# Putting the raw products of two units side by side in a fast-multiplication GeGLU kernel

## The chip, the cores and the metric

The kernel runs on one core of a Trainium2 chip. The time is microseconds of device time of one execution; the number quoted is the median of several executions. Before the change that was 541.36 us (three runs, 541.24 to 541.87).

## The reference

A gated feed-forward layer on 2048 tokens, all in bf16, with a model width of 1024 and an inner width of 3584:

```python
B, S, Dm, Df = 1, 2048, 1024, 3584
def reference(x, w_gate, w_up, w_down):
    g = jnp.einsum("bsd,df->bsf", x, w_gate)
    u = jnp.einsum("bsd,df->bsf", x, w_up)
    h = _gelu(g) * u                      # gelu with the tanh approximation
    return jnp.einsum("bsf,fd->bsd", h, w_down)
```

## The kernel before

The kernel does each matrix product as a 2x2 block product with seven block products in place of eight (Winograd's form). Two of the seven take the inputs as they are ("raw", bf16 operands). The other five take sums and differences of input blocks, kept in a 32-bit type (`f32r`): `s1`..`s4` and the cast `sa` of the weights, `t1`..`t4` and the cast `tb` of the tokens. The tokens go in two passes of 1024.

In the gate/up stage a "unit" makes 256 inner features of gate and of up. One block product is 2 x 4 matmuls (gate and up, four blocks of the contraction), so a unit is 16 raw and 40 32-bit matmuls, each 128x128 by 512 columns. A unit uses three pairs of PSUM banks (PSUM is the memory that matmuls write). Only unit 0 of the first pass is made plainly, with eight bf16 products. The raw products of the next unit are issued ahead, between this unit's `s4` product and its `sa` product:

```python
def raw_products(e, c, xT, w):
    for i in range(2):
        product(e[i], w[:, i, :KH, :P], [xT[0][:, k, :] for k in range(KH)], True)
    p1 = [snap(e[i], "p1") for i in range(2)]          # ScalarE copies
    for i in range(2):
        b21 = [xT[0][:, KH + k, :] for k in range(KH)]
        product(c[i], w[:, i, KH:, :P], b21, True)
    return p1

def unit(...):                                         # cut to TensorE's order
    product(e[i], s["s2"][i], t["t2"], False)          # each line for i in (0, 1)
    u2 = [snap(e[i], "u2") for i in GU]
    product(c[i], s["s1"][i], t["t1"], True)
    p5 = [snap(c[i], "p5") for i in GU]
    after_p5()                # GpSimd: s1..s4 of the next unit; weight load two ahead
    product(e[i], s["s3"][i], t["t3"], False)
    product(c[i], s["s4"][i], t["tb"], False)
    ahead_of_p4()             # raw products of the next unit
    product(e[i], s["sa"][i], t["t4"], False)
```

In both passes the down stage follows, with 392 matmuls of the same kind (112 bf16, 280 32-bit). One of its helpers fetches raw weights late in the stage:

```python
def fetch73(j):
    raw[3, j] = slot([P, 2, N], bf16, "raw")
    nc.sync.dma_start(out=raw[3, j], in_=wdn[:, :, j, N:])
```

All small tiles share one pool of 52 buffers (`slot`). DMAs are issued by SyncE. TensorE, VectorE, GpSimd and SyncE run in program order; ScalarE's order is chosen by the scheduler, except in the first unit.

Of the kernel before, what the change touches and what calls it, by code (L numbers as in the profile page):

```python
# [1 line left out]

# [8 lines left out]
def kernel(  # L11
# [23 lines left out]
    nc = tc.nc  # L35
    ENG = mybir.EngineType
# [3 lines left out]
    f32 = mybir.dt.float32  # L40
# [3 lines left out]
    ADD, SUB, MUL = ALU.add, ALU.subtract, ALU.mult  # L44
# [9 lines left out]
    NJ = NFB // 2  # L54
    N = 512
    NS = N // P
    NPASS = S // (2 * N)
    NU = NFB // 2
# [21 lines left out]
    wdn = w_down.rearrange("(kh j p) d -> p kh j d", kh=2, p=P)  # L80
# [14 lines left out]
    def new(eng, a, b, op, name, shape=None, dtype=None):  # L95
        t = slot(shape or [P, N], dtype or f32r, name)
        eng(t, a, b, op)
        return t
# [6 lines left out]
    def snap(ps, name):  # L105
        t = slot([P, N], f32, name)
        nc.scalar.copy(out=t, in_=ps)  # L107
        return t
# [8 lines left out]
    def load_w(u, queue=nc.sync):  # L117
        f0 = u * 2 * P
        w = wpool.tile([P, 2, NKB, 2 * P], bf16, name="w")
        for i, src in enumerate((w_gate, w_up)):  # L120
            queue.dma_start(
                out=w[:, i],
                in_=src[:, f0 : f0 + 2 * P].rearrange("(ko ki) f -> ki ko f", ki=P),
            )
        return w
# [38 lines left out]
    def pool_behind(tile):  # L164
        nc.gpsimd.tensor_copy(out=seen, in_=tile[:, :1].bitcast(f32))
# [6 lines left out]
    def make_s(w, eng):  # L172
        s = sums_s(w, eng)
        s.make("s1", "s2", "s3", "sa", "s4")
        return s

    def gelu(src):
        g = slot([P, N], f32, "g")
        nc.scalar.activation(g, src, ACT.Gelu_apprx_tanh)  # L179
        return g  # L180

    def times(fb, c, g, u):
        dve(hT[:, fb // NJ, fb % NJ, c, :], g, u, MUL)
# [14 lines left out]
    def add(ps, other):  # L198
        g = new(dve, ps[0], other[0], ADD, "sum", dtype=f32)
        dve(ps[1], ps[1], other[1], ADD)  # L200
        return g, ps[1]

    def unit(u, banks, xT, w, s, t, c11, after_p5, aside, keep, ahead_of_p4, behind_p4, snap_first):
        GU = range(2)
        e, c, d = banks
        aside(-2)
        g, up = c11()
        aside(-1)
        for i in GU:
            product(e[i], s["s2"][i], t["t2"], False)  # L210
        aside(0)
        keep(0, c[0])
        if snap_first:
            u2 = [snap(e[i], "u2") for i in GU]
            g = gelu(g)
        else:
            g = gelu(g)
        c11 = g, up
        if not snap_first:
            times(2 * u, 0, *c11)  # L220
            u2 = [snap(e[i], "u2") for i in GU]
        keep(1, c[0])
        keep(2, c[1])
        c = d
        for i in GU:
            product(c[i], s["s1"][i], t["t1"], True)
        p5 = [snap(c[i], "p5") for i in GU]
        after_p5()
        for i in GU:
            product(e[i], s["s3"][i], t["t3"], False)  # L230
        g, up = new(dve, e[0], p5[0], ADD, "sum", dtype=f32), banks[1][not snap_first]
        dve(up, e[1], p5[1], ADD)
        if snap_first:
            times(2 * u, 0, *c11)
        for i in GU:
            product(c[i], s["s4"][i], t["tb"], False)
        times(2 * u + 1, 1, gelu(g), up)
        aside(1)
        g, up = add(c, u2)
        ahead_of_p4()  # L240
        for i in GU:
            product(e[i], s["sa"][i], t["t4"], False)
        times(2 * u, 1, gelu(g), up)
        behind_p4()
        times(2 * u + 1, 0, gelu(e[0]), e[1])

# [6 lines left out]
    def fetch_wd(js):  # L253
        big = None
        for j in js:
            if j < NJ - 2:
                wraw[j] = [slot([P, Dm], bf16, "raw") for _ in range(2)]
            else:
                if big is None:
                    big = wpool.tile([P, 4, Dm], bf16, name="w")  # L260
                n = 2 * (j - NJ + 2)
                wraw[j] = [big[:, n + kh] for kh in range(2)]
            for kh in range(2):
                nc.sync.dma_start(out=wraw[j][kh], in_=wdn[:, kh, j, :])

    def keep_part(j, part, ps):
        ra, rb = wraw[j]
        if part == 0:
            made[j] = mpool.tile([P, 3, N], f32r, name="m")
        a = (ra[:, N:], rb[:, N:], rb[:, :N])[part]  # L270
        b = (ra[:, :N], made[j][:, 0], made[j][:, 1])[part]
        nc.scalar.copy(out=ps, in_=a)
        dve(made[j][:, part], ps, b, SUB)

    def keep_whole(j):
        ra, rb = wraw[j]
        m = made[j] = wpool.tile([P, 4, N], f32r, name="w")
        pool(m[:, 0], ra[:, N:], ra[:, :N], SUB)
        pool(m[:, 1], rb[:, N:], m[:, 0], SUB)
        pool(m[:, 2], rb[:, :N], m[:, 1], SUB)  # L280

    def store_made(j):
        nc.sync.dma_start(out=td[:, j], in_=made[j][:, :3].bitcast(f32))
# [28 lines left out]

    def fetch73(j):
        raw[3, j] = slot([P, 2, N], bf16, "raw")
        nc.sync.dma_start(out=raw[3, j], in_=wdn[:, :, j, N:])

    def make73(j):
        rr = raw[3, j]
# [147 lines left out]
    xT = new_x()  # L466
# [4 lines left out]
    w = load_w(1)  # L471
# [58 lines left out]
    def making(u):  # L530
        if u < 2 or u >= NU:
            return []
        return list(range(u - 2, NJ if u == NU - 1 else u - 1))

    for ip in range(NPASS):
        for u in range(1 if ip == 0 else 0, NU):
            js = making(u) if ip == 0 else []

            def prepare():
                nonlocal ahead  # L540
                if first:
                    pool_behind(t["t4"][-1])
                nxt["w"], nxt["s"] = ahead, None
                if u + 1 < NU:
                    nxt["s"] = make_s(ahead, pool)
                if u + 2 < NU:
                    ahead = load_w(u + 2)
                if len(js) == 1:
                    store_made(js[0])
                for j in js[1:]:  # L550
                    keep_whole(j)
                if ip == 0:
                    fetch_wd(making(u + 1))

            def keep(part, ps):
                if js:
                    keep_part(js[0], part, ps)

            def aside(part):
                if (ip, u) == (0, 1) and part < 0:  # L560
                    rest_of_0(part + 2)
                if part == 0 and "t4" not in t:
                    t.make("t4")

            def ahead_of_p4():
                if u + 1 < NU:
                    nxt["p1"] = raw_products(
                        even if u % 2 else odd, cc, xT, nxt["w"]
                    )

            def behind_p4():
                if "p1" in nxt:
                    nxt["c11"] = add(cc, nxt["p1"])

            def c11():
                return nxt.pop("c11", None) or add(cc, p1)

            e = odd if u % 2 else even
            p1 = nxt.pop("p1", None) or raw_products(e, cc, xT, w)
            first = (ip, u) == (0, 1)  # L580
            with tc.manual_schedule(engines={ENG.Activation}) if first else nullcontext():
                unit(
                    u, (e, cc, dd), xT, w, s, t, c11, prepare, aside, keep,
                    ahead_of_p4, behind_p4, first,
                )
            if u + 1 < NU:
                w, s = nxt["w"], nxt["s"]

        last = ip == NPASS - 1
        got, nxt = {}, {}  # L590

        def more(step):

            nonlocal ahead
            if last:
                return
            if step in (-1, 0, 2):
                store_made({-1: NJ - 3, 0: NJ - 2, 2: NJ - 1}[step])
            if step == 0:
                xT[:] = new_x()  # L600
            if step >= 24 and step % 2 == 0 and step // 2 - 12 < len(moves):
                c, ko = moves[step // 2 - 12]
                transposing(xT, c, ko, (2 * (ip + 1) + c) * N)
            if step == 50:
                got["w"], ahead = load_w(0), load_w(1)
            if step == 58:
                got["s"] = make_s(got["w"], dve)
            if step == 62:
                got["t"] = make_t(xT)

        down(ip, even + cc, dd + odd, last, more)
        even, odd, cc, dd = odd, even, dd, cc
        if not last:
            w, t, s = got["w"], got["t"], got["s"]

# [1 line left out]
_INS = ['x', 'w_gate', 'w_up', 'w_down']  # L617
# [26 lines left out]
```

## Time and profile before

| | before |
|---|---|
| time, median | 541.36 us |
| span of the profiled run | 539.9 us |
| PE (matmul) busy | 533.1 us, 99% |
| PEld (weight load) busy | 381.4 us, 71% |
| VectorE, ScalarE, GpSimd busy | 62%, 48%, 44% |
| waits of TensorE | one, 1.2 us at the start |

The first lines are from the page of the kernel before: part 1 (busy time, share, instructions) and part 4 (the chain that ended last).

```profile
PE 533.1 (99%) x2380; PEld 381.4 (71%) x2414; DVE 334.6 (62%) x524; ACT 260.0 (48%) x463; POOL 239.2 (44%) x215
...
PE 99%; issue 0%; ACT 0%; DVE 0%
```

TensorE is the bound. But a busy PE is not a PE at its peak, as matmuls overlap; the Trainium skill ("Perfetto Trace Analysis", section "Identifying the Most-Contended Engine") says the same and sends the reader to the share of peak FLOPs and that of weight loads (71% here). So look at the period. This is the chain of the kernel before in order of time (start us, length us, what):

```profile
82.92 0.07 issue
82.99 12.49 PE bank L111 x55
95.48 0.07 issue
95.55 12.49 PE bank L111 x55
108.04 0.07 issue
```

A unit takes 12.56 us. (x55 is not 56: this trace lacks 34 of 2414 matmul records, most of them the first bf16 matmul behind 32-bit ones. The 2414 weight loads are complete.) The timeline of PE shows the order within two units: start us, length us, operands, count.

```profile
145.79 3.40 PE L111 MATMUL bank<-xT,w 128*128 128x512 bf16 x15
148.84 2.19 PE L111 MATMUL bank<-t,sa 128*128 128x512 f32 x8
150.86 5.60 PE L111 MATMUL bank<-t,s 128*128 128x512 f32 x24
156.30 1.98 PE L111 MATMUL bank<-tb,s 128*128 128x512 f32 x8
158.35 3.40 PE L111 MATMUL bank<-xT,w 128*128 128x512 bf16 x15
161.40 2.19 PE L111 MATMUL bank<-t,sa 128*128 128x512 f32 x8
```

Each unit changes type twice: to bf16 ahead of `xT,w`, and back to 32-bit ahead of `t,sa`. Look at the two groups of eight: `tb,s` takes 1.98 us and `t,sa`, behind the change of type, 2.19 us. The start of the first record after a change is early, so the true cost is smaller than this difference; it comes from the spacing of starts in the single records, in the prediction below.

The weight loads by shape (count, busy us, mean ns, idle us) show where the two types part:

```profile
L111 PEld LDWEIGHTS bank<-t,s 128*128 128x128 f32 x648 | 121.6, 188 | 25.6
L111 PEld LDWEIGHTS <-w 128*128 128x128 bf16 x504 | 47.2, 98 | 58.2 <-issue 6.8
```

A 32-bit weight load takes 188 ns, a bf16 one 98 ns. The Trainium skill ("TensorE: Matmul & The Clock Gate", section "Weight-path perf modes — Fast Weight Load (FWL) and DoubleRow") states that the fast weight load is on for 128 weights of a type that is not FP32, measured at about 2x; this trace, which calls the 32-bit type f32, agrees with 1.9x.

### The profile page before, as it was taken

Reading aid. Unit: us, or ns where it says so; the run is one execution under the profiler, and the core shown is the slowest. Engines: PE = TensorE matmul, PEld = TensorE weight load, DVE = VectorE, ACT = ScalarE, POOL = GpSimd, SP = SyncE. Lnnn points to the kernel's source line nnn. Section 1 sums busy time; section 2 is a strip of 40 time slices with the busy share of each in tenths; the row PEclk is TensorE's granted clock in tenths of the full one; section 3 lists DMA queues with packets and bytes.
Section 4 is the critical chain, followed back from the end, with each engine's and each line's share of the span. In section 5 each row is a group of like instructions: output and inputs, shape, how many; then the busy total and the mean of one; then the engine's idle time right before and its main releaser. Section 6 shows DMA issues by size and latency. Waiting matters only on the chain.

```text
span 539.9 us, 7400 instructions
## 1 busy us (share of the span) xinstructions
PE 533.1 (99%) x2380; PEld 381.4 (71%) x2414; DVE 334.6 (62%) x524; ACT 260.0 (48%) x463; POOL 239.2 (44%) x215
## 2 busy tenths in 40 slices
PE   9999999999999999999999999999999999999997
PEld 5577777766777746888876767777777775488885
DVE  2986666666666895594945445555544459676730
ACT  2566666666666410255355555555555541114431
POOL 1169966677774400000097777777766600000000
PEclk9999999999999999999999999999999999999999
DMA  9776666766654899979673232233330079373751
GB/s 242 159 183 177 175 176 204 197 185 199 200 168 170 294 352 303 302 193 305 225 195 79 78 80 78 79 87 101 100 90 15 1 209 385 126 239 93 232 188 49
DMA packets 108134, 93.28 MB, mean 173 GB/s; under 512 B 17217, under 2 KB 92993, under 8 KB 108097
## 3 DMA queue, kind: packets, MB, share of 16 engines
q1 hardware_dynamic: 108096, 92.82, 59.4%
q8 instruction: 19, 0.31, 0.3%
q14 instruction: 19, 0.15, 0.1%
HBM read 74.45 MB, written 15.20 MB: 166 GB/s over the span
## 4 chain that ended last, share of the span: by engine, by line
PE 99%; issue 0%; ACT 0%; DVE 0%
PE bank L111 97%; PE bank L500 1%; PE bank L447 1%; ACT st L411 0%; DVE warm L431 0%
## 5 line engine op out<-in xcount | busy, mean ns | idle before, releaser
L93 POOL TENSOR_TENSOR s<-w 128x512 fp32r<-128x512 bf16 x102 | 119.9, 1196 | 166.2 <-DVE t L90 87.7
L111 PE MATMUL bank<-t,s 128*128 128x512 f32 x648 | 151.7, 390 | 0.0
L111 PEld LDWEIGHTS bank<-t,s 128*128 128x128 f32 x648 | 121.6, 188 | 25.6
L90 DVE TENSOR_TENSOR hT<-g,bank 128x512 bf16<-128x512 f32 x112 | 75.5, 685 | 67.7 <-ACT g L179 51.1
L107 ACT COPY p<-bank 128x512 f32<-128x512 f32 x124 | 70.5, 591 | 94.9 <-PE bank L111 94.8
L111 PE MATMUL bank<-xT,w 128*128 128x512 bf16 (+1 forms) x476 | 106.2, 375 | 1.9
L111 PEld LDWEIGHTS <-w 128*128 128x128 bf16 x504 | 47.2, 98 | 58.2 <-issue 6.8
L90 DVE TENSOR_TENSOR sum<-bank,p 128x512 f32<-128x512 f32 x54 | 37.1, 687 | 51.4 <-PE bank L111 51.4
L111 PE MATMUL bank<-q 128*128 128x512 f32 x240 | 58.9, 389 | 0.0
L111 PE MATMUL bank<-t,sa 128*128 128x512 f32 x216 | 58.7, 413 | 0.0
L93 POOL TENSOR_TENSOR s<-w,s 128x512 fp32r<-128x512 bf16 x50 | 57.8, 1181 | 0.0
L93 POOL TENSOR_TENSOR s<-s,w 128x512 fp32r<-128x512 f32 x50 | 57.0, 1160 | 0.0
L179 ACT ACTIVATE g<-sum 128x512 f32<-128x512 f32 x81 | 51.1, 630 | 8.5 <-DVE sum L90 7.4
L111 PE MATMUL bank<-tb,s 128*128 128x512 f32 x216 | 53.3, 389 | 0.0
L111 PEld LDWEIGHTS bank<-q 128*128 128x128 f32 x240 | 45.0, 188 | 9.4
L111 PE MATMUL bank<-raw,hT 128*128 128x512 bf16 x218 | 48.4, 379 | 0.3
L111 PEld LDWEIGHTS bank<-t,sa 128*128 128x128 f32 x216 | 40.7, 188 | 10.6
L107 ACT COPY u<-bank 128x512 f32<-128x512 f32 x62 | 35.9, 590 | 24.2 <-PE bank L111 21.8
L111 PEld LDWEIGHTS bank<-tb,s 128*128 128x128 f32 x216 | 40.5, 188 | 8.4
L102 ACT CAST tb<-raw 128x512 fp32r<-128x512 bf16 x28 | 17.2, 626 | 60.2 <-DMA raw<-in_w_down_dram 26.7
L90 DVE TENSOR_TENSOR q<-hT 128x512 fp32r<-128x512 bf16 x56 | 38.3, 685 | 4.1 <-PE bank L111 4.1
L179 ACT ACTIVATE g<-bank 128x512 f32<-128x512 f32 x31 | 18.6, 601 | 46.0 <-PE bank L111 45.7
(45 smaller groups left out, 464.0 us busy)
## 6 DMA issues: line engine op xcount, KB each, us to landing
raw<-in_w_down_dram SPq DMA_DIRECT2D x80, 256.0 KB, 4.8
q<-td SPq DMA_DIRECT2D x60, 256.0 KB, 4.9
w<-in_w_gate_dram SPq DMA_DIRECT2D x27, 512.0 KB, 5.9
w<-in_w_up_dram SPq DMA_DIRECT2D x27, 512.0 KB, 7.0
td<-m SPq DMA_DIRECT2D x12, 768.0 KB, 4.5
w<-td SPq DMA_DIRECT2D x6, 1024.0 KB, 9.8
out_dram<-st SPq DMA_DIRECT2D x32, 128.0 KB, 1.7
td<-w SPq DMA_DIRECT2D x2, 768.0 KB, 6.8
```

The source lines that it names most:

```text
L90: nc.vector.tensor_tensor(out=out, in0=a, in1=b, op=op)
L93: nc.gpsimd.tensor_tensor(out=out, in0=a, in1=b, op=op)
L102: nc.scalar.copy(out=t, in_=src)
L107: nc.scalar.copy(out=t, in_=ps)
L111: nc.tensor.matmul(ps, lhsT=lhs, rhs=rhs, start=start, stop=stop, skip_group_check=True)
L179: nc.scalar.activation(g, src, ACT.Gelu_apprx_tanh)
L447: nc.tensor.transpose(tp[:, ko, :], xn[i][:, ko * P : (ko + 1) * P], ident)
L500: nc.tensor.matmul(bank[3][:, :cols], lhsT=warm[:, :P], rhs=warm[:, :cols], start=True, stop=True)
```

## The change

The intent: issue the raw products of two units side by side, every other unit, so that TensorE changes type half as often. That needs a fourth pair of banks, so the pairs rotate (`E, K, C, F`). The raw weights must be there earlier, so their load moves ahead in the unit. ScalarE takes the program's order in the whole of gate/up. And two late fetches of each pass are split into two DMAs each. The core of the diff, with cuts marked:

```diff
@@ unit
-        if not snap_first:
-            times(2 * u, 0, *c11)
 ...
         g, up = add(c, u2)
+        times(2 * u, 1, gelu(g), up)
         ahead_of_p4()
         for i in GU:
             product(e[i], s["sa"][i], t["t4"], False)
-        times(2 * u, 1, gelu(g), up)
         behind_p4()
@@ fetch73
-        nc.sync.dma_start(out=raw[3, j], in_=wdn[:, :, j, N:])
+        for kh in (range(2),) if j < NJ - 2 else (range(1), range(1, 2)):
+            kh = slice(kh.start, kh.stop)
+            nc.sync.dma_start(out=raw[3, j][:, kh], in_=wdn[:, kh, j, N:])
@@ passes
+    E, K, C, F = odd, cc, dd, even
+    def raw_of(u, e):
+        p1 = raw_products(e, K, xT, loaded(u))
+        return lambda: finish_raw(u, K, p1)
 ...
+        with tc.manual_schedule(engines={ENG.Activation}):
 ...                                   # pass 1 begins with raw_of(0, F)() and raw_of(1, C)()
+                    if part == 0 and u + 2 < NU:
+                        loaded(u + 2)                  # was issued in after_p5
 ...
                 def ahead_of_p4():
-                    if u + 1 < NU:
-                        nxt["p1"] = raw_products(
-                            even if u % 2 else odd, cc, xT, nxt["w"]
-                        )
+                    if u % 2 and u + 1 < NU:
+                        raw_of(u + 1, F)()
+                        nxt["c11"] = raw_of(u + 2, C)
 ...
+                if u % 2 and not first:
+                    E, K, C = C, E, K
+                banks = (E, K, C) if u % 2 else (F, K, E)
```

More of the change, by code (lines that the diff above doesn't have):

```diff
@@ L1 @@
-from contextlib import ExitStack, nullcontext
+from contextlib import ExitStack
 import concourse.bass as bass
@@ L201, in add, with finish_raw, unit @@
         return g, ps[1]
-    def unit(u, banks, xT, w, s, t, c11, after_p5, aside, keep, ahead_of_p4, behind_p4, snap_first):
+    def finish_raw(u, c, p1):
+        g, up = add(c, p1)
+        times(2 * u, 0, gelu(g), up)
+    def unit(u, banks, s, t, late, after_p5, aside, keep, ahead_of_p4, behind_p4):
         GU = range(2)
@@ L206, in unit @@
         aside(-2)
-        g, up = c11()
+        g, up = late() if late else (None, None)
         aside(-1)
@@ L212, in unit @@
         keep(0, c[0])
-        if snap_first:
-            u2 = [snap(e[i], "u2") for i in GU]
-            g = gelu(g)
-        else:
+        u2 = [snap(e[i], "u2") for i in GU]
+        if late:
             g = gelu(g)
         c11 = g, up
-        if not snap_first:
-            times(2 * u, 0, *c11)
-            u2 = [snap(e[i], "u2") for i in GU]
         keep(1, c[0])
@@ L230, in unit @@
             product(e[i], s["s3"][i], t["t3"], False)
-        g, up = new(dve, e[0], p5[0], ADD, "sum", dtype=f32), banks[1][not snap_first]
+        g, up = new(dve, e[0], p5[0], ADD, "sum", dtype=f32), banks[1][not late]
         dve(up, e[1], p5[1], ADD)
-        if snap_first:
+        if late:
             times(2 * u, 0, *c11)
@@ L533, in making @@
         return list(range(u - 2, NJ if u == NU - 1 else u - 1))
-    for ip in range(NPASS):
-        for u in range(1 if ip == 0 else 0, NU):
-            js = making(u) if ip == 0 else []
-            def prepare():
-                nonlocal ahead
-                if first:
-                    pool_behind(t["t4"][-1])
-                nxt["w"], nxt["s"] = ahead, None
-                if u + 1 < NU:
-                    nxt["s"] = make_s(ahead, pool)
-                if u + 2 < NU:
-                    ahead = load_w(u + 2)
-                if len(js) == 1:
-                    store_made(js[0])
-                for j in js[1:]:
-                    keep_whole(j)
-                if ip == 0:
-                    fetch_wd(making(u + 1))
-            def keep(part, ps):
-                if js:
-                    keep_part(js[0], part, ps)
-            def aside(part):
-                if (ip, u) == (0, 1) and part < 0:
-                    rest_of_0(part + 2)
-                if part == 0 and "t4" not in t:
-                    t.make("t4")
-            def ahead_of_p4():
-                if u + 1 < NU:
-                    nxt["p1"] = raw_products(
-                        even if u % 2 else odd, cc, xT, nxt["w"]
-                    )
-            def behind_p4():
-                if "p1" in nxt:
-                    nxt["c11"] = add(cc, nxt["p1"])
-            def c11():
-                return nxt.pop("c11", None) or add(cc, p1)
-            e = odd if u % 2 else even
-            p1 = nxt.pop("p1", None) or raw_products(e, cc, xT, w)
-            first = (ip, u) == (0, 1)
-            with tc.manual_schedule(engines={ENG.Activation}) if first else nullcontext():
@@ new lines, with loaded, prepare, keep @@
+    E, K, C, F = odd, cc, dd, even
+    def loaded(u):
+        if u not in ws:
+            ws[u] = load_w(u)
+        return ws[u]
+    def raw_of(u, e):
+        p1 = raw_products(e, K, xT, loaded(u))
+        return lambda: finish_raw(u, K, p1)
+    for ip in range(NPASS):
+        with tc.manual_schedule(engines={ENG.Activation}):
+            if ip == 0:
+                ws = {1: w, 2: ahead}
+                late = lambda: add(cc, nxt["p1"])
+            else:
+                raw_of(0, F)()
+                raw_of(1, C)()
+            for u in range(1 if ip == 0 else 0, NU):
+                js = making(u) if ip == 0 else []
+                first = (ip, u) == (0, 1)
+                def prepare():
+                    if first:
+                        pool_behind(t["t4"][-1])
+                    if u + 1 < NU:
+                        nxt["s"] = make_s(loaded(u + 1), pool)
+                    if len(js) == 1:
+                        store_made(js[0])
+                    for j in js[1:]:
+                        keep_whole(j)
+                    if ip == 0:
+                        fetch_wd(making(u + 1))
+                def keep(part, ps):
+                    if js:
+                        keep_part(js[0], part, ps)
+                def aside(part):
+                    if first and part < 0:
+                        rest_of_0(part + 2)
+                    if part == 0 and u + 2 < NU:
+                        loaded(u + 2)
+                    if part == 0 and "t4" not in t:
+                        t.make("t4")
+                def ahead_of_p4():
+                    if u % 2 and u + 1 < NU:
+                        raw_of(u + 1, F)()
+                        nxt["c11"] = raw_of(u + 2, C)
+                def behind_p4():
+                    if "c11" in nxt:
+                        nxt.pop("c11")()
+                if u % 2 and not first:
+                    E, K, C = C, E, K
+                banks = (E, K, C) if u % 2 else (F, K, E)
@@ L582 @@
                 unit(
-                    u, (e, cc, dd), xT, w, s, t, c11, prepare, aside, keep,
-                    ahead_of_p4, behind_p4, first,
-                )
-            if u + 1 < NU:
-                w, s = nxt["w"], nxt["s"]
+                    u, banks, s, t, late if first else None, prepare, aside, keep,
+                    ahead_of_p4, behind_p4,
+                )
+                s = nxt.pop("s", None)
         last = ip == NPASS - 1
@@ L592, in more @@
         def more(step):
-            nonlocal ahead
             if last:
@@ L604, in more @@
             if step == 50:
-                got["w"], ahead = load_w(0), load_w(1)
+                ws.clear()
+                ws.update({n: load_w(n) for n in range(2)})
             if step == 58:
-                got["s"] = make_s(got["w"], dve)
+                got["s"] = make_s(ws[0], dve)
             if step == 62:
                 got["t"] = make_t(xT)
-        down(ip, even + cc, dd + odd, last, more)
-        even, odd, cc, dd = odd, even, dd, cc
+        down(ip, F + K, C + E, last, more)
+        E, K, C, F = K, E, F, C
         if not last:
-            w, t, s = got["w"], got["t"], got["s"]
+            t, s = got["t"], got["s"]
 _INS = ['x', 'w_gate', 'w_up', 'w_down']
```

## The prediction

> **What bounds the kernel.** TensorE. The page gives PE 533.1 of 539.9 us busy, the chain that ended last is 99% PE, and the waits view has one wait of PE, 1.2 us at the start. So I read the spacing of matmul starts in the instruction records. A bf16 matmul of 512 columns follows the last one after 215.8 ns (the Trainium skill, "TensorE: Matmul & The Clock Gate", section "Back-to-back issue gap", gives N/2.4 + 2.5 = 216; the trace agrees). A 32-bit one follows after 226.7 ns: its weight load takes 188 ns plus a 39 ns gap, a bf16 load 97 ns. A unit is 16 bf16 and 40 32-bit matmuls: 16 x 215.8 + 40 x 226.7 = 12.52 us. The chain shows a period of 12.56 us. The missing 0.04 us is at changes of type: after bf16 to 32-bit, the next 12 matmuls take 25.5 ns more than their spacing; going back costs 13.5 ns.
>
> **What the change does.** No matmul, copy, add or GELU is removed. Raw blocks (16 bf16 matmuls each) are paired: in pass 0 the 12 separate blocks become 6, in pass 1 the 14 become 7. So 13 pairs of type changes go: 13 x 39 ns = 0.51 us, all on the critical path. The rest moves work of engines with slack: ScalarE (48% busy), VectorE (62%), GpSimd (44%). ScalarE's program order, laid out with durations (copy 0.59, cast 0.62, GELU 0.63, add or multiply 0.69 us), still empties each bank before TensorE returns; tightest is the second raw block's cc-role bank, read until about 1.0 us before it is written. The later unit's raw weights are needed about 8.9 us after their load is issued; landing takes 5.9 to 7.0 us (page, part 6). Splitting two 256 KB fetches per pass adds four DMAs and removes no TensorE wait, as none is there.
>
> **The danger** is GpSimd. It makes a unit's four sums in 9.4 us (8 x 1.17). Before, in steady state, it starts just after the s4 product (pass 0) or the s3 product (pass 1) of the unit before, waiting for a buffer, and in pass 0 finishes s2 only 0.5 us before TensorE needs it. After, an even unit has no raw block: from P5 to the next s2 are 24 matmuls, 5.4 us, and s1 and s2 take 4.7 us. Released only after s4, it would hold TensorE about 2.9 us per pair: some 37 us. I expect it to run further ahead: a pair lasts 25 us and holds 19 us of GpSimd work.
>
> **Time.** 541.36 - 0.51 = 540.9 us; 8 in 10: 540.2 to 542.2. Faster by over 2%: 1%. Within 2%: 92%. Slower by over 2%: 7%.
>
> **What would show it.** Right: bf16-to-32-bit changes fall from 29 to 16; a pair of units takes 25.08 us instead of 25.12; PE has no new wait; the remaining changes still cost 25.5 and 13.5 ns. Wrong: TensorE waits on GpSimd's s tiles at the head of odd units, or on ScalarE or VectorE before the second raw block, or on the later raw block's weight load.
>
> **What would make it wrong.** Another assignment of the 52 shared buffers, which ties GpSimd or the in-order ScalarE to a late event; the start of pass 0, where VectorE is busy without a break until about 37 us; the start of pass 1, where the second raw block follows the last copies of the down stage.

## The result

The kernel after took 540.57 us (median of 6 runs, 540.25 to 540.93), beside 541.62 us of the kernel before (6 runs, 541.24 to 542.11). The ratio is 0.9981, with a 95% interval of 0.9968 to 0.9994. A ratio here is the mean time of one kernel's fast runs over that of the other's of the same rounds, so it is not quite the ratio of the medians. The change saves a fifth of a per cent: within 2%, as predicted.

The page of the kernel after, the same parts:

```profile
PE 534.5 (99%) x2414; PEld 382.3 (71%) x2414; DVE 341.8 (63%) x524; ACT 261.4 (49%) x463; POOL 237.7 (44%) x215
...
PE 99%; ACT 0%; DVE 0%; issue 0%
```

The timeline of PE in the kernel after, an even unit and an odd one:

```profile
141.42 5.60 PE L111 MATMUL bank<-t,s 128*128 128x512 f32 x24
146.86 1.98 PE L111 MATMUL bank<-tb,s 128*128 128x512 f32 x8
148.68 1.98 PE L111 MATMUL bank<-t,sa 128*128 128x512 f32 x8
150.49 5.60 PE L111 MATMUL bank<-t,s 128*128 128x512 f32 x24
155.93 1.98 PE L111 MATMUL bank<-tb,s 128*128 128x512 f32 x8
157.75 7.08 PE L111 MATMUL bank<-xT,w 128*128 128x512 bf16 x32
164.48 0.80 PE L111 MATMUL bank<-t,sa 128*128 128x512 f32 x2
```

The raw matmuls now come 32 at a time, and the `t,sa` group of the even unit has no change ahead of it and takes 1.98 us like its neighbours. The records of the last bf16 matmuls before a change, at 64.13, 89.21 and 114.29 us, are 25.08 us apart: the pair's period that was predicted. TensorE has no new wait; its only one is still the 1.2 us at the start.

To compare traces to hundredths of a us, I cut each into parts:

- the start, up to the first 32-bit matmul of unit 1. Nothing in it was changed, and it differs from execution to execution: the first matmul of unit 0 began anywhere from 6.73 to 8.14 us in the 12 profiles. TensorE's first matmuls speed up at another moment each time: the spacing of the 128-column transposes falls from 107 to 56 ns at 7.0 us in the trace before and at 6.6 us in the one after;
- the stretch, from there to the end of the last matmul;
- the tail, from there to the end of the span.

| | start of unit 0 | stretch | tail | changes to 32-bit |
|---|---|---|---|---|
| before | 7.88 us | 511.36 us | 3.45 us | 29 |
| after | 7.71 us | 510.84 us | 3.17 us | 16 |

The stretch is shorter by 0.52 us: the 0.51 us of the prediction. The tail is shorter by 0.28 us, which nobody predicted. Together that is 0.80 us, or a ratio of 0.9985, well inside the measured interval. The remaining 0.17 us of the two profiles is the start.

### The profile page after: what moved, and what is told of

Its sections match the earlier page's. It is cut to its first block, busy times and chain, and to the rows that moved or that the text cites. A ratio compares the mean times of both kernels' runs of the same rounds, so it can differ in the third digit from the quotient of the medians.

```text
span 538.9 us, 7457 instructions
## 1 busy us (share of the span) xinstructions
PE 534.5 (99%) x2414; PEld 382.3 (71%) x2414; DVE 341.8 (63%) x524; ACT 261.4 (49%) x463; POOL 237.7 (44%) x215
## 4 chain that ended last, share of the span: by engine, by line
PE 99%; ACT 0%; DVE 0%; issue 0%
PE bank L111 98%; PE bank L501 1%; PE bank L448 1%; ACT st L412 0%; DVE warm L432 0%
## 5 line engine op out<-in xcount | busy, mean ns | idle before, releaser
L93 POOL TENSOR_TENSOR s<-w 128x512 fp32r<-128x512 bf16 x102 | 118.4, 1183 | 163.4 <-PE bank L111 113.7
L111 PEld LDWEIGHTS bank<-t,s 128*128 128x128 f32 x648 | 121.6, 188 | 25.5
L111 PE MATMUL bank<-xT,w 128*128 128x512 bf16 (+1 forms) x504 | 109.6, 376 | 0.0
L90 DVE TENSOR_TENSOR hT<-g,bank 128x512 bf16<-128x512 f32 x112 | 76.8, 687 | 17.9 <-ACT g L179 5.0
L111 PE MATMUL bank<-t,sa 128*128 128x512 f32 x216 | 55.9, 401 | 0.0
L90 DVE TENSOR_TENSOR bank<-bank,p 128x512 f32<-128x512 f32 x54 | 37.7, 699 | 9.1 <-PE bank L111 6.2
```

The costliest lines, as they stand in the source:

```text
L90: nc.vector.tensor_tensor(out=out, in0=a, in1=b, op=op)
L93: nc.gpsimd.tensor_tensor(out=out, in0=a, in1=b, op=op)
L111: nc.tensor.matmul(ps, lhsT=lhs, rhs=rhs, start=start, stop=stop, skip_group_check=True)
```

## The experiments

Two theories were to be tested. The first says that the gain in the stretch is the changes of type and nothing else. Its rivals say that the rotation, ScalarE's order or the loads had a part. For the tail there was no theory at first.

The stretch and the tail come from one profile of each kernel; the times are medians. The recorded expectations of e1 to e4 count from the first matmul of unit 0, which is 17.17 us more in both kernels (528.53 and 528.01 us). As that piece is not the same in every profile (17.28 us in e2, 17.36 to 17.39 us in the three bf16 kernels), I count from the later point: take 17.17 us off the sizes in those four texts. Waits in brackets are read from the spacing of single matmul records; they are too short for the view of waits.

| kernel | stretch | tail | changes | time | before, same rounds | ratio (95%) |
|---|---|---|---|---|---|---|
| e1_apart | 511.83 (0.46 a wait) | 3.18 | 28 | 540.73 | 541.38 | 0.9988 (0.9975 to 1.0002) |
| e2_mixed | 513.00 | 3.17 | 100 | 542.57 | 541.38 | 1.0020 (1.0007 to 1.0033) |
| e3_actsched | 511.14 (0.27 a wait) | 3.18 | 16 | 540.40 | 541.38 | 0.9982 (0.9970 to 0.9995) |
| e4_whole | 510.92 (0.09 a wait) | 3.44 | 16 | 541.18 | 541.38 | 0.9995 (0.9983 to 1.0008) |
| e5_before_split | 511.36 | 3.17 | 29 | 541.60 | 541.39 | 1.0002 (0.9990 to 1.0015) |
| e6_two_more | 511.20 (0.32 a wait) | 3.32 | 16 | 540.75 | 541.39 | 0.9983 (0.9969 to 0.9996) |
| e7_pool | 510.84 | 3.18 | 16 | 540.28 | 541.39 | 0.9977 (0.9964 to 0.9991) |
| e8_bf16 | 498.39 | 3.18 | 2 | 528.47 | 541.39 | 0.9757 (0.9743 to 0.9770) |
| e10_before_bf16 | 498.41 | 3.44 | 2 | 528.26 | 541.26 | 0.9757 (0.9742 to 0.9771) |
| e9_bf16_all | 492.26 | 3.18 | 0 | 522.21 | 541.26 | 0.9644 (0.9628 to 0.9660) |

The times cannot tell 0.3 us apart, as the start alone varies by 1.4 us. The parts of the traces can: kernels with the same matmul order agree in the stretch to 0.1 us, once single waits are taken out. All results passed the comparison with the reference.

### The pair taken apart (e1_apart)

```diff
                         raw_of(u + 1, F)()
-                        nxt["c11"] = raw_of(u + 2, C)
+                        nxt["c11"] = lambda: raw_of(u + 2, C)()   # now behind the sa product
```

> Kernel after, but the second raw block stands behind the sa.t4 product of the odd unit instead of in front of it: the pairing is undone, bank rotation, ScalarE order, early weight load and split fetches stay. Measure: from the start of the first gate/up matmul (unit 0) to the end of the last matmul, 528.53 us before, 528.01 us after. Theory (changes of operand type are all that was paid for): 12 more pairs of changes, 28 bf16-to-32-bit changes in place of 16, 12 x 39 ns = 0.47 us more, so 528.48 us; a pair of units back at 25.12 us. Rival (the gain comes from the rotation, the ScalarE order or the earlier loads): 528.0 us, pair at 25.08.

The trace has 28 changes and pairs of units at 25.12 us again. One unit differs, at 104 to 107 us: ScalarE waited for a DMA, and TensorE then twice for ScalarE, 0.46 us more than the unit's usual time. ScalarE's waits in that stretch (us in total, times, longest us):

```profile
ACT bank L271 <- DMA raw<-in_w_down_dram: 2.4, 1, 2.4
ACT g L179 <- DVE sum L90: 1.4, 1, 1.4
```

Without that one the stretch is 511.37 us, beside 511.31 expected (510.84 + 0.47). So all of the gain leaves with the pairing, although rotation, order and loads stay. The lone wait is a risk of program order: a copy that waits for a late DMA stands in ScalarE's queue in front of the copies that TensorE needs. One execution shows it; I did not look for how often it comes.

### More changes of type (e2_mixed)

```diff
-        ahead_of_p4()
-        for i in GU:
-            product(e[i], s["sa"][i], t["t4"], False)
+        ahead_of_p4(one_of_p4)      # one sa matmul behind every four raw ones
+        while todo_p4:
+            one_of_p4()
 ...                                # raw_products calls one_of_p4 behind each four
```

> Kernel after, but in each of the 12 odd units with a pair of raw blocks the eight 32-bit matmuls of the sa.t4 product are put one by one behind each group of four bf16 matmuls: 8 changes to 32-bit in place of 1, 84 more in all, same matmuls. Theory, if each change costs its full 39 ns however few 32-bit matmuls follow: +3.3 us in the matmul stretch (531.3 us). If only the change back (13.5 ns) and the first 32-bit matmul (3.5 ns) are paid when the 32-bit run is one matmul long: +1.4 us (529.4 us). Rival, that changes of type cost nothing and the gain had another source: 528.0 us.

The stretch grew by 2.16 us for 84 changes, 25.7 ns each: between the two sizes that I had set out. The timeline of PE in this kernel shows the pattern:

```profile
83.11 1.04 PE L111 MATMUL bank<-xT,w 128*128 128x512 bf16 x4
83.80 0.58 PE L111 MATMUL bank<-t,sa 128*128 128x512 f32 x1
84.23 1.04 PE L111 MATMUL bank<-xT,w 128*128 128x512 bf16 x4
84.92 0.58 PE L111 MATMUL bank<-t,sa 128*128 128x512 f32 x1
85.34 1.04 PE L111 MATMUL bank<-xT,w 128*128 128x512 bf16 x4
```

Four bf16 matmuls and one 32-bit one take 1.113 us; 4 x 215.8 + 226.7 ns would be 1.090. So a round trip with a single 32-bit matmul costs 23 ns: about 12 ns in the change back itself and 11 ns in the second bf16 matmul, which starts 227 ns after the first. The 39 ns of a long 32-bit run include a slow recovery: its spacings after the change are 224, 231, 236, 228, 232 and 231 ns before they settle at 226.7. Behind the last change of such a unit of e2 the recovery is longer, with nine spacings (229, 233, 236, 224, 231, 236, 228, 233 and 231 ns), and costs about 19 ns more; with seven round trips of 23 ns that makes the 180 ns that each of the 12 units grew by, so 25.7 ns is a mean of two prices. The price of a change is thus real and depends on the length of what follows and of what went before. What in the array causes the recovery, no run here shows.

### ScalarE's order given back to the scheduler (e3_actsched)

```diff
-        with tc.manual_schedule(engines={ENG.Activation}):
+        with nullcontext():         # and around unit(): manual for the first unit only
```

> Kernel after with the program order on ScalarE given up for all gate/up units but the first, as it was before (the scheduler orders it). Theory: ScalarE has slack, TensorE waits for nothing either way, matmul stretch 528.0 us, no wait of TensorE. Rival (the program order is a part of the gain, or is needed by the pairing): over 528.3 us, with waits of TensorE on ScalarE or on VectorE behind it.

The stretch is 511.14 us (the rival's line is 511.13), but the excess is one wait of 0.27 us at 206.6 us, in the down stage of pass 0, which does not belong to ScalarE: TensorE waited there for the last raw weights, issued at 197.5 us and landed at 207.0 us. Without it the stretch is 510.87 us, that of the kernel after. The same wait, 0.09 and 0.32 us long, is in the profiles of e4 and e6, and in no other. In the kernel after the data landed at 206.4 us, and no wait shows. It is a close race. The time from issue to landing was 9.4 to 9.5 us in all these kernels; it is the issue that varies, 172.8 to 173.0 us after the start of the stretch in e3, e4 and e6 and 172.1 in the kernel after. Why SyncE issued later there stays open. The pairing makes the race closer: TensorE comes to these weights 182.46 us after the start of the stretch in e5, which has the order of before, and 182.22 us in the kernel after.

So ScalarE's program order neither helps nor hurts the paired order here.

### The fetches whole again (e4_whole)

```diff
-        for kh in (range(2),) if j < NJ - 2 else (range(1), range(1, 2)):
+        for kh in (range(2),):
```

> Kernel after with the two late weight fetches of each pass whole (256 KB each) as before. Theory (they are off the critical path): 528.0 us, no wait of TensorE. Rival (the new order of the queue or of the buffers made them late, and the split repaired it): TensorE waits in the third stage of down for the products of j = 12 or 13, some tenths of a us or more a pass.

TensorE did not wait for these weights, as I expected. But the tail was 3.44 us, as before the change, and not 3.17. That made the theory of the tail. These are SyncE's instruction records after the last matmul's end (us from that end; the numbers are semaphores):

```
before (e4_whole alike)              after
0.65  issues the last store (105)    0.65  issues the last store (109)
2.37  it lands                       2.34  it lands
2.38  waits for 105, 104             1.03  waits for 105, 104
2.45  waits for 106, 103             1.09  waits for 106, 103
2.51  waits for 107, 101             1.15  waits for 107, 101
2.57  waits for 108, 100             1.22  waits for 108, 100
2.63  waits for 109, 110             2.35  waits for 109, 110
2.70  drain                          2.42  drain
```

At the end of the program SyncE waits for all semaphores, two at a time, some 62 ns each. In the kernel before, the last store has a semaphore that stands first in that list, so the other four waits come after the store has landed. With four more DMAs in the program, the last store has the semaphore four places on, the last in the list, and the other four waits are done while it flies. Four waits of 62 ns are 0.25 us of the 0.28; the other 0.03 us is the landing (2.37 and 2.34 us). The store takes 1.7 us from issue to landing. (The Trainium skill, "DMA: Bandwidth & Descriptors", section "Anatomy of one DMA — SWDGE (gpsimd) path", puts a fixed cost of about 2.0 us on a DMA of another issuing path; this store, 128 KB, took less.)

### The split alone, in the kernel before (e5_before_split)

The same three lines of the split, put into the kernel before. Nothing else.

> Kernel before with nothing but the split of the two late weight fetches of each pass, so four more DMAs in all and no other edit. Read so far: from the end of the last matmul to the end of the span it is 3.45 us in the kernel before and with whole fetches (e4), 3.17 us in all kernels with the split. At the end SyncE waits for its DMA semaphores two at a time, 62 ns each; the last store's semaphore is the first of the list in the first two, the last in the others. Theory (four more DMAs turn the rotation of semaphores by four): tail 3.17 us, first 32-bit matmul to last matmul unchanged at 511.36 us, 29 changes of type, so 0.28 us less than before. Rival (the tail is shorter because of something in the new gate/up order, or by chance): tail 3.45 us.

The stretch is 511.36 us, exactly that of before, and the tail 3.17 us. The last store has semaphore 109. The time shows no gain (1.0002, with an interval that holds the expected 0.9995), which is what one can ask of a time with this spread.

### Two more DMAs in place of four (e6_two_more)

```diff
-        for kh in (range(2),) if j < NJ - 2 else (range(1), range(1, 2)):
+        for kh in (range(2),) if j < NJ - 1 else (range(1), range(1, 2)):
```

> Kernel after with only the last of the two fetches of each pass split, so two DMAs more than before in place of four. Theory of the rotation: the last store gets the semaphore two places earlier in the list of the end, two more pairs of waits come behind its landing, tail 3.17 + 2 x 0.06 = 3.30 us; matmul stretch from the first 32-bit matmul 510.84 us as after. Rival: 3.17 us, or 3.45 us.

The last store has semaphore 107. Two waits come behind its landing, at 2.43 and 2.50 us, and the tail is 3.32 us, beside 3.30 expected. The size of the fetch is therefore not the point; the count of DMAs is. The stretch has the wait of e3, and is 510.88 us without it.

### GpSimd delayed (e7_pool)

```diff
-                        nxt["s"] = make_s(loaded(u + 1), pool)
+                        nxt["s"] = sn = sums_s(loaded(u + 1), pool)
+                        sn.make("s1")
+                        if u % 2 == 0:
+                            pool(warm, warm, warm, ADD)
+                        sn.make("s2", "s3", "sa", "s4")
```

> Kernel after with one more GpSimd operation (128x512, on a tile that nobody reads) between s1 and s2 of every odd unit's sums; it does nothing for the result. In kernel after GpSimd finishes s2 of an odd unit 0.63 us before TensorE takes it in pass 0 (steady state) and about 2.4 us before in pass 1. Theory (this is the tightest wait that the change made): TensorE waits at the head of the odd units of pass 0, about 1.1 - 0.6 = 0.5 us in each of four to five, 2 to 2.5 us in all, and hardly in pass 1. Rival (GpSimd has slack everywhere, since it is busy only 44%): no wait, 510.84 us.

Nothing happened: 510.84 us and no wait. I had read the trace wrongly. GpSimd's timeline in this kernel shows the added operation between `s1` and `s2`:

```profile
82.17 2.27 POOL L93 TENSOR_TENSOR s<-w 128x512 fp32r<-128x512 bf16 x2 [3.67 <-DVE hT L90]
84.41 1.04 POOL L93 TENSOR_TENSOR warm<-warm 128x512 bf16<-128x512 bf16 x1
85.40 2.27 POOL L93 TENSOR_TENSOR s<-s,w 128x512 fp32r<-128x512 f32 x2
```

These sums are for unit 7, as the added operation is in odd units' sums only. TensorE takes unit 7's `s2` at 99.7 us; `s2` is done at 87.7 us. The margin is 12 us, not 0.6. I had paired each set of sums with the next `s2` product in time; it is for the one after that. Counting the sets from the start shows it in the kernel before as well. There the last set of pass 1 (POOL's last four lines of that trace) begins at 420.07 us and is for unit 13:

```profile
420.07 2.29 POOL L93 TENSOR_TENSOR s<-w 128x512 fp32r<-128x512 bf16 x2 [3.51 <-PE bank L111]
422.31 2.27 POOL L93 TENSOR_TENSOR s<-s,w 128x512 fp32r<-128x512 f32 x2
```

Its `s2` is done at 424.6 us, and unit 13's first product starts at 439.5 us.

### No type to change (e8_bf16, e10_before_bf16, e9_bf16_all)

In e8 the sums of gate/up are kept in bf16 in the kernel after; in e10 the same edit is made in the kernel before; in e9 the sums of the down stage are bf16 too.

```diff
-        t = slot(shape or [P, N], dtype or f32r, name)     # sums s and t
+        t = slot(shape or [P, N], dtype or bf16, name)
-                "tb": lambda q: [cast(hi[1][k], "tb") for k in K],
+                "tb": lambda q: [cast(hi[1][k], "tb", None, bf16) for k in K],
 ...                                   # sa alike; e9: td, made, q and their casts alike
```

> Kernel after with the sums s and t of gate/up kept in bf16 in place of 32 bit, so that no gate/up matmul is 32-bit: the same matmuls, other numerics (the result may miss the reference; that is part of the question). Theory (a 32-bit matmul takes 226.7 ns because of its 188 ns weight load, a bf16 one 215.8 ns, a change of type 39 ns): 27 x 40 x 10.9 ns = 11.8 us and 14 changes of 39 ns = 0.5 us less, so about 528.2 us, unless GpSimd (9.4 us a unit, even units now 8.6 us long) begins to hold TensorE. Rival (spacing is not set by the type): no change.

> Kernel before (raw blocks apart, whole fetches) with the sums of gate/up in bf16, as e8 is kernel after with them. Without 32-bit matmuls in gate/up there are no changes of type for the pairing to save. Theory: the stretch from the first product of sums to the last matmul is the same as in e8, 498.4 us, and only the 0.28 us at the end differ (tail 3.45 us). Rival (the pairing, rotation or order saves something besides the changes of type): about 0.5 us more than e8, 498.9 us.

> Kernel e8 with the sums of the down stage in bf16 too (and the made weights that go through DRAM): no 32-bit matmul left. Theory: 560 matmuls of down at 215.8 in place of 226.7 ns, 6.1 us, and 2 changes of type, so a stretch of about 492.2 us and 522.3 us in all, if the result still passes. Rival (down is held by something else, such as DMA or VectorE, once TensorE is quicker): less gain, with waits of TensorE in down.

All three came out as expected to 0.2 us: 498.39 (the estimate of 12.3 us less gives 498.5), 498.41 and 492.26 us. e8 and e10 differ by 0.02 us in the stretch, although one has the raw blocks in pairs and the other has not. With no change of type to save, the pairing saves nothing; that is the sharpest test of the theory. The weight loads of e9:

```profile
L111 PEld LDWEIGHTS <-s 128*128 128x128 bf16 x864 | 84.5, 98 | 101.9
L111 PEld LDWEIGHTS <-w 128*128 128x128 bf16 x504 | 49.3, 98 | 57.6
L111 PEld LDWEIGHTS <-q 128*128 128x128 bf16 x448 | 43.9, 98 | 52.8
```

All loads take 98 ns, PEld is busy 45% of the span, and the view of waits has nothing of TensorE's matmuls but the 1.2 us at the start. In these three kernels the type changed the weight load and the spacing together, so they do not tell whether the slower load is what makes the 32-bit spacing 11 ns longer. e9 beats both kernels, with 522.21 us. It buys this with other numerics: sums rounded to bf16. How much of the tolerance it used was not measured.

## Why the prediction was right, and where it was not

**Right: the bound and the term.** TensorE bound the kernel, and the changes of type were the only thing on the critical path that the pairing touched. Predicted: 29 to 16 changes, a pair at 25.08 us, 0.51 us. Measured: 16, 25.08, and 0.52 us in the stretch; the changes that remain still cost 25 to 26 and 13.5 ns. e1, e2 and e10 show the cause: put the changes back and the gain goes; add changes and time is added; remove all of them and pairing is worth 0.02 us. The time alone would not have shown this: the stated range of 2.0 us holds a gain of nothing as well as one of 0.51 us.

**Right: ScalarE, VectorE and the banks.** No new wait of TensorE came, and e3 shows that ScalarE's order was free. The bank that the prediction called tightest was read until 0.83 us before TensorE wrote it (13 pairs, 0.827 to 0.832), beside the estimate of about 1.0.

**Wrong: the split.** The prediction said that the split "removes no TensorE wait, as none is there". True, but it looked at TensorE only. The split shortened the end of the program by 0.28 us, by moving the last store's semaphore (e4, e5, e6). The part of the gain that the traces attribute is therefore 0.80 us, and the sum in the prediction lacked this term.

**Wrong: the danger.** "In pass 0 finishes s2 only 0.5 us before TensorE needs it" is false: GpSimd worked a unit further ahead. In the kernel before it had 13.1 us in hand in the steady state of pass 0 and 14.9 in pass 1; in the kernel after no less than 12.7 and 14.3. Only the first sets of a pass are closer: 2.1 us for unit 2 of pass 0 before, 5.6 after. The expectation that it would "run further ahead" was right by luck, as it rested on the wrong pairing of sums and products. e7 tested the false margin and found no wait.

**A size that depends on context.** 39 ns for a change of type holds for the runs of this kernel. With a single 32-bit matmul between bf16 ones it is 23 ns.

What is left open: the cause of the slow recovery after a change to 32-bit; whether the weight load sets the 32-bit spacing; why the issue ahead of the wait near 206 us was late in three kernels; and, in times, anything smaller than about 0.1%.

## What to carry to other kernels

When an engine is busy all the time and waits for nothing, read the spacing of its instructions by kind, and at each change of kind: here the 32-bit type cost 11 ns on each of some 1,600 matmuls, about 18 us, and the changes of type that the edit removed only half a us. Look at what happens after the last instruction too, as an edit that only changes the number of DMAs can move the end. And before you call a wait tight, count which consumer a product is for.

## What the Trainium skill lacked or had wrong

- "TensorE: Matmul & The Clock Gate", section "Back-to-back issue gap", gives a sustained spacing of about 131 ns for 512 columns in a stream of weight loads and matmuls. No run here came near it: bf16 matmuls in such streams are 215.8 ns apart, in e9 from the first unit to the end, which agrees with the formula of N/2.4 + 2.5 ns that the section gives for an isolated matmul.
- The same page has no spacing for the 32-bit type used here: a matmul of 512 columns every 226.7 ns, with a weight load of 188 ns and a gap of 39 ns before the next one.
- The same page does not say that a change of operand type costs anything: 25.5 ns to 32-bit (spread over about seven matmuls) and 13.5 ns back in long runs, 23 ns for both around a single 32-bit matmul.
- No page has SyncE's list at the end of the program: it waits for its semaphores two at a time, 62 ns each, so the last store's place in that list of five waits is worth up to 4 x 62 ns = 0.25 us.
